# A guard on the softmax of a fused attention and feed-forward kernel: sums judged on GpSimd, and a second path behind a branch

## The chip, the cores and the metric

The kernel runs on one core of a Trainium2 chip. The metric is the device time of one execution in microseconds (us). Engines: TensorE (PE; its weight loads are PEld), VectorE (DVE), ScalarE (ACT), GpSimd (POOL) and SyncE (SP), each with its own stream of instructions, which it takes strictly in order. [...] A trailing q (SPq, POOLq) is the sequencer of an engine, which issues DMAs and handles semaphores.

## The reference

Attention over q, k and v (8 batches, 12 heads, 448 tokens, 64 columns a head), and then a feed-forward layer of width 2048 on the 3584 tokens with 768 columns:

```
scores = (1/8) * q @ k.T
scores = scores - max(scores, over the keys)
attn = exp(scores);  attn = attn / (sum(attn, over the keys) + 1e-9)
x = attn @ v                       # heads put side by side: 3584 x 768
h = x @ w_in;  g = h * sigmoid(h);  out = g @ w_out
```

q, k and v are 0.1 times standard normal draws, so every score is close to 0, every exponential close to 1, and every sum close to 448. Subtracting the maximum changes nothing in exact arithmetic; it keeps the exponentials in range where scores are large.

## The kernel before, in words

**Tiling.** The attention is cut into 24 units (`units`): 8 batches times 3 groups of 4 heads. A unit's keys and queries are loaded (POOL's queue), turned by DVE, multiplied to scores by TensorE (L404), and turned to exponentials in fp16 by ScalarE (`expo`, L442), without the maximum taken off. Two neighbouring units share one tile of exponentials. The sums of the exponentials come from TensorE by products with ones (L495); `inverse` (L541 to L562) turns them on VectorE (L546), takes the reciprocal (L554) and spreads it back (L560); `norm` (L576) multiplies it into the product of exponentials and values (L479). So 24 units times 14 query blocks of 32 give 24 x 14 = 336 inverse sums on each of 128 partitions. In `before`, an inverse lies in a small tile of two rotating buffers (tag `inv`).

**Feed-forward.** Batches 0 to 5 run its first half through `ffn1` (L394, the helper `wide`) with tanh on ScalarE (L602) and a product on VectorE (L640), for the last two of them only in part; batches 4 and 5, and 6 and 7, go in pairs through `pair_product` (L729). Products there are made from sums and differences of blocks: 7 products in the place of 8 (m = 1 to 7 in the order 1, 5, 6, 2, 3, 7, 4). The combined inputs are tiles `sx` (`combine_x`, L676: for b0 = 4 and b0 = 6, m = 1 to 4), the combined weights tiles `tw` or `V` (`combine_w_in`, L709). VectorE adds results in PSUM (`pair_add`, L745: three of them a block, called u, w and v), ScalarE takes copies (L742) and applies silu (L762). The second half runs in the same way over 14 quads of rows (`product`, L394 and for the last quads L799; `combine_g`, L781; `add_in`, L876; `add_out`, L881; `take_out`, L863). The results lie in tiles `ost` and are stored from SyncE's queue, in the last stage from ScalarE's too (L855, and L837 for the last quad). The last columns are copied by `take_half`, by VectorE (L872) and ScalarE (L870).

**Buffers.** Tiles of one tag share a number of buffers. When a tag has no free one, the first instruction that writes the new tile waits until the last reader of an old tile is done. The tag `E` has nine (NE = 9), each of 128 partitions x 3584 bytes. They hold exponentials during the attention; after its end two `sx` of b0 = 4, the four `sx` of b0 = 6 and three `tw` take them.

**Order.** The order of all instructions is written by a planner in the kernel (`class Order`). It plays the kernel through with costs of its own on its own clock (`od.now`), picks for each engine what runs next, and puts a function into `od.out` with the planned time. At the end the list is sorted by time and then by place in the list, and the functions are called; each emits its instructions into the streams:

```
    for _, _, fn in sorted(od.out, key=lambda x: x[:2]):
        fn()
```

The scheduler of the layer below is told to keep this order (`manual_schedule`). TensorE's work goes through `on_pe`; `inv_op` is the list of the planned reciprocals, and `inv_op[-1].done` the planned end of the last. When the program is closed (L1769) the engines drain, meet, and the semaphores are cleared.

Of the kernel before, what the change touches and what calls it, by code (L numbers as in the profile page):

```python
# [10 lines left out]
FP32 = mybir.dt.float32  # L11
AF = mybir.ActivationFunctionType
ALU = mybir.AluOpType
# [74 lines left out]
class Order:  # L88
# [34 lines left out]
    def on_pe(self, op, mode):  # L123
        if mode == "full" and self.attention:
            mode, op.strips = "cols", True
        gap = SWITCH if mode != self.mode else 0.0
        self.mode = mode
        op.busy += gap
        self.start(op)

    def load(self, rows, row_bytes, emit, ring=None, gate=None):
# [52 lines left out]
        return soon  # L184


@with_exitstack
def kernel(
    ctx: ExitStack,
# [4 lines left out]
    moe_w_in: bass.AP,  # L194
    moe_w_out: bass.AP,
    out: bass.AP,
):
    nc = tc.nc

    B, NH, S, D = q.shape  # L200
    DM = NH * D
    DFF = moe_w_in.shape[1]
    HG = 4
    NG = NH // HG
    TPP = S // 32
# [7 lines left out]
    NFF = DFF // 128  # L213
# [16 lines left out]
    NE, NX3, NT_ = 9, 8, 2  # L230
    NXT = 3 * NX3
    NSG, NTMP, NOST = 3, 3, 4
    attn_scale = 1.0 / (D**0.5)

    const = ctx.enter_context(tc.tile_pool(name="const", bufs=1))
    sb = ctx.enter_context(tc.tile_pool(name="sb", bufs=1))
    ps = ctx.enter_context(tc.tile_pool(name="ps", bufs=1, space=bass.MemoryType.PSUM))
# [20 lines left out]
    ones = const.tile([128, 32], FP16, name="ones")  # L258
# [14 lines left out]
    w_out_t = const.tile([128, NFF, DM], FP16, name="w_out_t")  # L273
# [23 lines left out]
    rawk, rawq, KT, QT, E, T, acc, rdn_t, xT, g_t, ost_t = ({} for _ in range(11))  # L297
    sT_t, inv_t = {}, {}
# [242 lines left out]
    def inverse(ns, step, i=0):  # L541
        g0, g1 = units[ns[0]][2:]
        shape = [128, g1 - g0, 32]
        if step == 0:
            sT_t[ns[0]] = sb.tile(shape, FP32, name=f"sT_{ns[0]}", tag="rdn", bufs=2)
            nc.vector.transpose(  # L546
                out=sT_t[ns[0]],
                in_=acc[(ns[0], 0)][:, 0 : 32 * (g1 - g0)].rearrange("p (g i) -> p g i", i=32),
            )
        elif step == 1:  # L550
            inv_t[ns[0]] = sb.tile(
                shape[:2] + [len(ns)], FP32, name=f"inv_{ns[0]}", tag="inv", bufs=2
            )
            nc.vector.reciprocal(  # L554
                out=inv_t[ns[0]], in_=sT_t[ns[0]][:, :, 0 : 32 : 32 // len(ns)]
            )
        else:
            n = ns[i]
            rdn_t[n] = sb.tile(shape, FP32, name=f"rdn_{n}", tag="rdn", bufs=2)
            nc.vector.transpose(  # L560
                out=rdn_t[n], in_=inv_t[ns[0]][:, :, i : i + 1].to_broadcast(shape)
            )  # L562
# [47 lines left out]
    G = const.tile([128, NFF, 2 * S], FP16, name="G")  # L610
# [282 lines left out]
    units = []  # L893
# [3 lines left out]
    NU = len(units)  # L897

    od = Order(SHY)
# [68 lines left out]
    for n in range(NB0 + NG, NU):  # L968
        b, hg = units[n][:2]
# [4 lines left out]
    turned = {"n": 0}  # L974
# [43 lines left out]
    inv_op, norm_op = [], []  # L1018
# [615 lines left out]
    def after_sums(ns, op, nq):  # L1634
        wide = nq / 960.0 + 0.15
        turn = od.add(
            Op("DVE", wide, lambda: inverse(ns, 0), [op] + inv_op[-1:] + norm_op[-4:], B_INV, then=m_ring.back(spot[("a", ns[0], 0)]))
        )
        inv = od.add(Op("DVE", 0.2 + 0.01 * len(ns), lambda: inverse(ns, 1), [turn], B_INV))
        inv_op.append(inv)  # L1640
        for i, n in enumerate(ns):
            rdn_op[n] = [
                od.add(
                    Op(
                        "DVE",
                        wide,
                        lambda i=i: inverse(ns, 2, i),
                        [inv] + norm_op[-4:],
                        B_INV,
                    )  # L1650
                )
            ]
# [24 lines left out]
    def spare():  # L1677
        ready = [(t, 2 * i) for t, i in s_ring.free if t <= od.now]
        ready += [(t, 4 + i) for t, i in m_ring.free if t <= od.now]
        return min(ready)[1] if ready else None  # L1680

    while True:
# [48 lines left out]
        at = spare()  # L1731
        if warm["on"] and at is not None and od.free["PE"] <= od.now and wait > 0.06 and od.now > 0.9:
            each = mm(128) if od.now > COLD else 0.07 if od.now > 6.5 else 0.107
            n = max(1, int((wait - 0.06) / each), int(wait / each + 0.9) * (od.now < 14.0))
            n += MORE0 * (6.5 < od.now < COLD) + 2 * (COLD < od.now < 14.0)
            if warm.pop("first", None):
                n = FIRST
            od.on_pe(Op("PE", n * each, lambda n=n, at=at: run_zeros(n, at)), "full")
        od.now = min(later)
        assert od.now < 2000.0  # L1740
    assert not (qk_seq or av_seq or moe or any(od.wait.values()) or od.pool)
    for _, _, fn in sorted(od.out, key=lambda x: x[:2]):
        fn()


# [28 lines left out]
```

## Time and profile before

| | |
|---|---|
| median of 3 runs | 382.34 us (381.79 to 382.81) |
| the profiled execution | 382.55 us, its span 380.5 us |
| instructions in the span | 12933 |
| PE busy | 373.5 us (98%) |
| DVE busy | 280.2 us (74%) |
| ACT busy | 257.6 us (68%) |
| POOL busy | 85.3 us (22%) |
| granted TensorE clock | 0.999 |

The span goes from the first to the last instruction of the profile; the execution's own time holds 2.05 us more around it. The page has the busy time of each engine, the span in 40 slices of 9.5 us with the busy share of each in tenths, the DMA queues with packets and bytes, the chain of waits that ended last, and groups of instructions by line. The timeline has one line for each run of like instructions: start, duration, engine, line, operation, output and inputs, and in brackets how long the engine had idled before and what released it. Instructions of one engine are pipelined, so a line's duration can reach over the next one's start.

### The profile page before, as it was taken

How to read it: one execution, taken by the hardware profiler on the slowest of the kernel's cores; microseconds unless marked ns; L12 is line 12 of the kernel's file. 1: busy time of each engine (PE TensorE's matmuls, PEld its weight loads, DVE VectorE, ACT ScalarE, POOL GpSimd, SP SyncE). 2: the span in 40 equal slices, each digit the busy share in tenths (PEclk: the TensorE clock that was granted, in tenths of full speed). 3: DMA queues.
4: the chain of work that ended last, by engine and by line, in shares of the span. 5: the costliest groups of instructions: out<-in, count | busy, mean ns of one | idle time of the engine just before them, and what ended most of it. 6: DMA issues, size and time to landing. Idle time of an engine off the chain costs nothing.

```text
span 380.5 us, 12933 instructions
## 1 busy us (share of the span) xinstructions
PE 373.5 (98%) x5516; PEld 192.0 (50%) x5516; DVE 280.2 (74%) x560; ACT 257.6 (68%) x425; POOL 85.3 (22%) x155
## 2 busy tenths in 40 slices
PE   7999999999999999999999999999999999999995
PEld 6433455444455444445444454555556655555653
DVE  5679799999996868997869978789866334556331
ACT  4998854787867787967788787728762259883221
POOL 7537616306042603324240500000000000000000
PEclk9999999999999999999999999999999999999999
DMA  7999999936558843739391712120002330001433
GB/s 103 198 206 190 204 211 183 152 74 91 72 96 135 147 67 44 106 72 169 80 150 26 93 24 72 34 54 0 1 2 69 84 98 2 0 1 39 106 88 103
DMA packets 35961, 34.66 MB, mean 91 GB/s; under 512 B 11968, under 2 KB 35136, under 8 KB 35904
## 3 DMA queue, kind: packets, MB, share of 16 engines
q0 software_dynamic: 25200, 22.82, 40.4%
q1 hardware_dynamic: 10176, 10.53, 10.1%
q8 instruction: 43, 0.70, 0.8%
q10 hardware_dynamic: 528, 0.49, 0.5%
q14 instruction: 14, 0.11, 0.1%
HBM read 45.61 MB, written 11.01 MB: 149 GB/s over the span
## 4 chain that ended last, share of the span: by engine, by line
PE 92%; ACT 3%; DMA 2%; DVE 1%; issue 1%; POOLq 0%
PE banks L394 53%; PE banks L729 15%; PE banks L404 11%; PE banks L479 10%; ACT E L442 3%; PE banks L495 2%; PE banks L799 1%; DMA out_dram<-ost 1%; DMA rk<-in_k_dram 1%; PE banks L1673 0%; DVE ost L881 0%; DVE T L453 0%; PE banks L515 0%; DVE KT L377 0%; DVE rq L387 0%
## 5 line engine op out<-in xcount | busy, mean ns | idle before, releaser
L442 ACT ACTIVATE E<-banks 128x896 f16<-128x896 f32 x168 | 144.1, 919 | 41.2 <-PE banks L404 40.9
L394 PE MATMUL banks<-xT,w_in_t 128*32 128x448 f16 (+1 forms) x1446 | 90.5, 353 | 0.0
L394 PE MATMUL banks<-w_out_t,G 128*32 128x384 f16 (+1 forms) x968 | 67.4, 327 | 0.0
L394 PEld LDWEIGHTS <-G 128*32 128x32 f16 (+1 forms) x1240 | 47.0, 97 | 34.0 <-issue 6.5
L394 PEld LDWEIGHTS <-w_in_t 128*32 128x32 f16 (+1 forms) x1446 | 42.2, 97 | 43.2 <-issue 12.7
L340 POOL DMA_DIRECT2D V<-in_v_dram x84 | 46.0, 560 | 56.0 <-PE banks L479 42.9
L404 PE MATMUL banks<-rq,KT 32*128 32x448 f16 (+1 forms) x768 | 52.1, 362 | 1.5 <-ACT E L442 0.9
L602 ACT ACTIVATE th<-banks 128x448 f16<-128x448 f32 x72 | 37.2, 553 | 15.0 <-PE banks L394 12.5
L640 DVE SCALAR_TENSOR_TENSOR G<-th,banks 128x448 f16<-128x448 f16 (+1 forms) x72 | 39.9, 572 | 4.9 <-ACT th L602 4.5
L863 ACT COPY ost<-banks 128x384 f32<-128x384 f32 x41 | 19.7, 485 | 33.3 <-PE banks L394 17.5
L394 PE MATMUL banks<-D,S 128*32 128x384 f16 (+1 forms) x544 | 38.1, 327 | 0.0
L762 ACT ACTIVATE G<-banks 128x448 f16<-128x448 f32 (+3 forms) x72 | 33.8, 555 | 5.3 <-DVE banks L745 3.5
L479 PE MATMUL banks<-E,V 128*32 128x448 f16 x672 | 35.7, 353 | 0.0
L576 DVE SCALAR_TENSOR_TENSOR xT<-banks,rdn 128x448 f16<-128x448 f32 x48 | 29.2, 618 | 5.6 <-PE banks L479 3.0
L745 DVE TENSOR_TENSOR banks<-banks,q 128x448 f32<-128x448 f32 x28 | 17.6, 632 | 16.6 <-PE banks L729 15.4
L394 PEld LDWEIGHTS <-S 128*32 128x32 f16 (+1 forms) x544 | 20.6, 97 | 14.7 <-issue 3.1
L404 PEld LDWEIGHTS <-KT 32*128 32x128 f16 (+1 forms) x768 | 12.4, 96 | 30.7 <-issue 27.3
L453 DVE TENSOR_TENSOR T<-E,E 128x1792 f16<-128x1792 f16 x22 | 23.8, 1080 | 5.6 <-ACT E L442 5.5
L453 DVE TENSOR_TENSOR T<-T,E 128x1792 f16<-128x1792 f16 x22 | 23.9, 1085 | 5.2 <-ACT E L442 5.0
L317 POOL DMA_DIRECT2D rq<-in_q_dram x25 | 14.0, 559 | 59.8 <-PE banks L404 47.9
L479 PEld LDWEIGHTS <-V 128*32 128x32 f16 x672 | 17.0, 97 | 16.0 <-issue 3.9
L729 PEld LDWEIGHTS <-w_in_t 128*128 128x128 f16 x168 | 16.4, 98 | 15.2
(156 smaller groups left out, 401.3 us busy)
## 6 DMA issues: line engine op xcount, KB each, us to landing
out_dram<-ost SPq DMA_DIRECT2D x200, 48.0 KB, 1.6
rk<-in_k_dram POOLq DMA_DIRECT2D x23, 224.0 KB, 5.4
rq<-in_q_dram POOLq DMA_DIRECT2D x23, 224.0 KB, 5.4
w_out_t<-in_moe_w_out_dram POOLq DMA_DIRECT2D x4, 768.0 KB, 12.6
V<-in_v_dram POOLq DMA_DIRECT2D x42, 64.0 KB, 3.9
V<-in_v_dram POOLq DMA_DIRECT2D x42, 48.0 KB, 4.6
w_in_t<-in_moe_w_in_dram POOLq DMA_DIRECT2D x3, 512.0 KB, 11.2
w_in_t<-in_moe_w_in_dram POOLq DMA_DIRECT2D x6, 256.0 KB, 5.9
```

The costliest lines, as they stand in the source:

```text
L340: nc.gpsimd.dma_start(out=v_of(b, hg0)[32 * x : 32 * (x + 1), at, 0:count, :], in_=v[b, hs].rearrange("h (i g) d -> i h g d", g=TPP)[:, :, ...
L394: nc.tensor.matmul(out=out[at], lhsT=lhsT[:, at], rhs=rhs, **flags)
L404: nc.tensor.matmul(out=pS[p0 : p0 + 32 * (x1 - x0), h % 2, at : at + nq], lhsT=KT[(b, hg)][32 * h : 32 * (h + 1), c, x0:x1, :, e], rhs=QT[ ...
L442: nc.scalar.activation(out=E[(n, w)][0:kr, 2 * y : 2 * y + 2, 0:nk], in_=pS_t[(n, w, y)][0:kr, :, 0:nk], func=AF.Exp, scale=attn_scale,)
L453: nc.vector.tensor_tensor(out=T[n], in0=T[n] if step else E[(n, 0)], in1=E[(n, step + 1)], op=ALU.add,)
L479: nc.tensor.matmul(out=a[32 * h : 32 * (h + 1), 0:nq], lhsT=w, rhs=e[k0:k1, h, at : at + nq], start=start, stop=stop,)
L576: nc.vector.scalar_tensor_tensor(out=x3(b, cc)[:, cc % 3, 32 * g0 : 32 * g1], in0=acc[(n, part)][:, 0:nq], scalar=0.5, in1=rdn_t[n].rearra ...
L602: nc.scalar.activation(out=th, in_=h_t[(b, f, t0)][:, 0 : t1 - t0], func=AF.Tanh)
L640: nc.vector.scalar_tensor_tensor(out=dst[:, f, at + lo : at + hi], in0=th_t[(b, f, t0)][:, lo - t0 : hi - t0], scalar=1.0, in1=h_t[(b, f, ...
L729: nc.tensor.matmul(out=pp_t[(f, PBANK[m])], lhsT=w[:, c, :], rhs=a[:, c, :], start=(c == 0 and m in (1, 6, 5)), stop=(c == 2), skip_group_ ...
L762: nc.scalar.activation(out=o, in_=a, func=AF.Silu, scale=2.0)
L863: nc.scalar.copy(out=ost(qd, i, j), in_=bank(qd, m))
```

## The change

The former kernel function becomes `without_maximum`. The new top function allocates a pool `guard` with a flag of one int32, runs `without_maximum`, which hands back the flag's value as read into a register of every engine, and then stands an `If`: where the value isn't 1, all engines run `with_maximum`, which computes the whole result a second time in fp32, with each query's maximum taken off, and writes `out` again. The inputs of this case give a flag of 1.

In `without_maximum` the inverses of all units are kept in one array `inv_all` of 128 x 336 fp32 in the place of the rotating tiles. `judge` works in three steps, put into the planner's list 20, 28 and 36 us behind the planned end of the last reciprocal: step 0 marks on GpSimd which inverses lie between 1/60000 and 1/64 (two comparisons and a product, 128 x 336 each); step 1 takes the least mark of each partition on VectorE and moves the 128 values into one row by a DMA from GpSimd; step 2 takes the least of the row on VectorE and turns it to the int32 flag on GpSimd. Its scratch tile takes a buffer of the tag `E`. The flag is read (`values_load`, on all engines) at the planned time of the last call of `on_pe`, behind it in the list. The planner's own run isn't changed.

The diff, cut to its core; `with_maximum` is a plain unrolled loop over batches and heads, of which some lines stand here:

```diff
@@ -126,6 +126,7 @@
         gap = SWITCH if mode != self.mode else 0.0
         self.mode = mode
         op.busy += gap
+        self.pe_last = self.now
         self.start(op)
 
     def load(self, rows, row_bytes, emit, ring=None, gate=None):
...
+JUDGED = 20.0
+SUM_LOW, SUM_HIGH = 64.0, 6.0e4
...
+    nc = tc.nc
+    guard = ctx.enter_context(tc.tile_pool(name="guard", bufs=1))
+    flag = guard.tile([1, 1], mybir.dt.int32, name="flag")
+    fine = without_maximum(tc, q, k, v, moe_w_in, moe_w_out, out, guard, flag)
+    with tc.If(fine != 1, preferred_fallthrough_block=False):
+        with_maximum(tc, q, k, v, moe_w_in, moe_w_out, out)
+
+
+def judge(nc, spare, inv, flag, step):
+    n = inv.shape[1]
+    low, high = spare[:, 0:n], spare[:, n : 2 * n]
+    row, one = spare[:, 2 * n : 2 * n + 1], spare[0:1, 2 * n + 1 : 2 * n + 2]
+    line = spare[0:1, 2 * n + 2 : 2 * n + 130]
+    if step == 0:
+        nc.gpsimd.tensor_scalar(
+            out=low, in0=inv, scalar1=1.0 / SUM_LOW, scalar2=None, op0=ALU.is_le
+        )
+        nc.gpsimd.tensor_scalar(
+            out=high, in0=inv, scalar1=1.0 / SUM_HIGH, scalar2=None, op0=ALU.is_ge
+        )
+        nc.gpsimd.tensor_tensor(out=low, in0=low, in1=high, op=ALU.mult)
+    elif step == 1:
+        nc.vector.tensor_reduce(out=row, in_=low, axis=mybir.AxisListType.X, op=ALU.min)
+        nc.gpsimd.dma_start(out=line, in_=row)
+    else:
+        nc.vector.tensor_reduce(out=one, in_=line, axis=mybir.AxisListType.X, op=ALU.min)
+        nc.gpsimd.tensor_copy(out=flag, in_=one)
+
+
+def with_maximum(ctx, tc, q, k, v, moe_w_in, moe_w_out, out):
+    nc = tc.nc
+    B, NH, S, D = q.shape
+    DFF, DM = moe_w_in.shape[1], NH * D
+    NQ, G, NFF = S // 112, S // 32, DFF // 128
...
+    def turned(src, b, h, name):
+        raw = two.tile([32, G, D], FP32, name=f"raw_{name}", tag=f"raw_{name}")
+        nc.sync.dma_start(out=raw, in_=src[b, h].rearrange("(g i) d -> i g d", i=32))
+        t = two.tile([32, 2, S], FP32, name=f"t_{name}", tag=f"t_{name}")
+        for i in range(2):
+            for g in range(G):
+                nc.vector.transpose(
+                    out=t[:, i, 32 * g : 32 * (g + 1)], in_=raw[:, g, 32 * i : 32 * (i + 1)]
+                )
+        return t
...
+    for b in range(B):
+        xT = one.tile([D, NH, S], FP32, name="g_xT", tag="g_xT")
+        for h in range(NH):
+            qT, kT = turned(q, b, h, "q"), turned(k, b, h, "k")
...
+            for c in range(NQ):
...
+                m = two.tile([112, 1], FP32, name="g_m", tag="g_m")
+                nc.vector.tensor_reduce(
+                    out=m, in_=s[:, 0:S], axis=mybir.AxisListType.X, op=ALU.max
+                )
+                nc.sync.dma_start(out=row[:, 112 * c : 112 * (c + 1)], in_=m)
...
+                e = two.tile([112, S], FP32, name="g_e", tag="g_e")
+                nc.scalar.activation(out=e, in_=s[:, 0:S], func=AF.Exp, scale=1.0 / D**0.5)
+                for o, w in ((x, vt[:, c]), (total, ones)):
+                    nc.tensor.matmul(
+                        out=o[:, 0:S], lhsT=w, rhs=e, start=(c == 0), stop=(c == NQ - 1)
+                    )
...
+        for f in range(NFF):
...
+            nc.scalar.activation(out=gate[:, f], in_=hid[:, 0:S], func=AF.Silu)
...
+            nc.sync.dma_start(out=out[at : at + 112], in_=o)
...
+def without_maximum(
...
+    inv_all = guard.tile([128, NG * B, TPP], FP32, name="inv_all")
...
         elif step == 1:
-            inv_t[ns[0]] = sb.tile(
-                shape[:2] + [len(ns)], FP32, name=f"inv_{ns[0]}", tag="inv", bufs=2
-            )
+            b, hg = units[ns[0]][:2]
+            at = NG * b + hg
+            whole = inv_all[:, at : at + len(ns)].rearrange("p n g -> p (n g)")
+            inv_t[ns[0]] = whole.rearrange("p (g n) -> p g n", n=len(ns))
...
     assert not (qk_seq or av_seq or moe or any(od.wait.values()) or od.pool)
+    spare_t = []
+
+    def judged(step):
+        if step == 0:
+            spare_t.append(
+                sb.tile([128, 2 * NU * TPP + 130], FP32, name="judge", tag="E", bufs=NE)
+            )
+        judge(nc, spare_t[0], inv_all.rearrange("p n g -> p (n g)"), flag, step)
+
+    read = []
+    why = "compared only, no address is made of it"
+
+    def read_flag():
+        read.append(nc.values_load(flag, skip_runtime_bounds_check_because=why))
+
+    od.out.append((od.pe_last, len(od.out), read_flag))
+    for step in range(3):
+        at = inv_op[-1].done + JUDGED + 8.0 * step
+        od.out.append((at, len(od.out), lambda step=step: judged(step)))
     for _, _, fn in sorted(od.out, key=lambda x: x[:2]):
         fn()
+    return read[0]
```

## The prediction

> **What bounds the kernel now.** I read the page's parts 1 to 3 first, then the chain of waits, then the timeline by engine from 245 us to 290 us (where the sums are judged) and from 372 us on (where the flag is read), and last the rows of the line that closes the program, L1769.
>
> The page:
>
> ```profile
> PE 373.5 (98%) x5516; PEld 192.0 (50%) x5516; DVE 280.2 (74%) x560; ACT 257.6 (68%) x425; POOL 85.3 (22%) x155
> ...
> POOL 7537616306042603324240500000000000000000
> ...
> q8 instruction: 43, 0.70, 0.8%
> ```
>
> TensorE is busy 98% of the span, and in the chain of waits it holds 92%. So a microsecond of TensorE idleness anywhere before the last stage is a microsecond of the result; it is not won back. GpSimd does nothing after slice 23 (its last DMA issue ends near 217 us). The third line is the code itself: with q14 it makes 57 packets and 0.81 MB for 12,933 instructions, 63 bytes each. The engines fetch their code by DMA while they run, in pieces of 0.70 MB / 43 = 16.3 KB, about 260 instructions.
>
> The timeline of VectorE and of TensorE around 274 us, where the change's buffer matters:
>
> ```profile
> 272.92 0.63 DVE L745 TENSOR_TENSOR banks<-banks,q 128x448 f32<-128x448 f32 x1
> 273.46 0.85 DVE L676 TENSOR_TENSOR sx<-xT,sx 128x1344 f16<-128x1344 f16 x1
> 275.02 0.63 DVE L745 TENSOR_TENSOR banks<-banks,q 128x448 f32<-128x448 f32 x1 [0.71 <-PE banks L729]
> ```
> ```profile
> 274.82 0.73 PE L729 MATMUL banks<-sx,tw 128*128 128x448 f16 x3
> 275.39 0.73 PE L729 MATMUL banks<-xT,w_in_t 128*128 128x448 f16 x3
> 275.95 0.73 PE L729 MATMUL banks<-xT,tw 128*128 128x448 f16 x3
> ```
>
> The L676 at 273.46 is the last of the tiles `sx` (the one for b0 = 6, m = 4), and VectorE idles 0.71 us behind it. The L745 at 275.02 ends at 275.65, and TensorE's third group starts 0.30 us later, on the bank that it read.
>
> The end of the kernel, first the timeline, then the rows of L1769:
>
> ```profile
> 374.43 3.01 SPq L837 DMA_DIRECT2D out_dram<-ost  x3
> 374.94 1.48 PE L799 MATMUL banks<-D,G 128*128 128x192 f16 x16
> 375.14 0.48 ACT L863 COPY ost<-banks 128x384 f32<-128x384 f32 x1 [2.12 <-PE banks L799]
> 376.52 0.36 DVE L872 COPY ost<-banks 128x192 f32<-128x192 f32 x1 [2.12 <-DMA out_dram<-ost]
> 376.91 0.32 ACT L870 COPY ost<-banks 128x192 f32<-128x192 f32 x1 [1.29 <-DVE ost L872]
> 377.26 0.66 ACTq L837 DMA_DIRECT2D out_dram<-ost  x1
> ```
> ```profile
> L1769 SPq EVENT_SEMAPHORE  x10: 17/28/28, 377.5 to 380.4; - x10
> ...
> L1769 SPq DRAIN  x3: 7/7/7, 379.6 to 379.9; - x3
> ```
>
> TensorE ends at 376.42, two copies follow, the last store is issued until 377.92, and SyncE waits for its landing until 379.6. From there to 380.45 the engines meet twice and the semaphores are cleared: a closing round of 0.85 us.
>
> The profiled execution took 382.55 us (2.05 us around its span of 380.5), 0.21 us above the median of 382.34. I sum against 382.55 and take 0.21 off at the end.
>
> **The change, part by part.**
>
> *Inverse kept in one array.* The 14 reciprocals (L554, 0.31 us) write 28 or 14 columns elsewhere; number and shape stay. Two rotating buffers go, and no wait stood on them (the list of waits has none for `inv`). Cost 0.
>
> *Three GpSimd operations on 128x336 f32.* The program order puts them 20 us behind the last inverse, but GpSimd is in no queue with anything then, so they start when their inputs and their buffer allow: the last reciprocal ends at 248.4, the E buffers of the last unit are free when its products (L479) end at 252.9. No such operation is in the trace. Bounds for one: 0.10 us (GpSimd's memset of one column) and 1.26 us (twice VectorE's 0.63 us for 128x448 f32). I take 0.7, so 2.1 us, 253 to 255. Nobody waits for them before 276. Cost 0 by that row. Beside VectorE work at the same time both bounds stay: nothing, or up to 1.0 us, if the L709s at 252.98 to 254.4 (three, 0.55 us each) are held up by them and VectorE, which has no idle time from 251.5 to 261.5, hands half on. I take 0 and keep 1.0. [...]
>
> *The buffer of these operations.* It is an E buffer (nine of them), and this is the first term that I count. After the last exponential nine tiles take E buffers, in the order of their first writes: sx of b0 = 4 twice (243.70, 245.47), two tw (253.9, 260.4), sx of b0 = 6 (263.04, 268.32), a tw (269.09), sx (270.92, 273.46). Nine for nine: none waits. Judge's tile is asked for at 248.4 + 20 = 268.4 by the planner's clock, some 2 to 5 us ahead of the last two. So it makes ten, and the last, the L676 at 273.46, gets the buffer of the first, which is free only when the last product with it is done: that is the triple sx,tw at 274.82, ending at 275.55. Then L676 starts at 275.6 instead of 273.46, and behind it in VectorE's order the L745 starts 0.77 later (the step from one L676 to the next operation at 263.04), at 276.37 instead of 275.02. It ends at 277.0, TensorE's group of 275.95 starts at 277.15 or up to 277.3: a hole of 1.2 to 1.35 us. VectorE then has the idle 1.01 us ahead of 279.16 to catch up, so nothing adds to it. **I count 1.2 us**; bounds 0 (the tile comes after 273.46, or finds a free buffer) and 1.35.
>
> *Step 1: a reduction of 128x336 f32 on VectorE and a DMA of 128x4 bytes from GpSimd.* Between 0.31 (L554, 28 columns) and 0.63 us (L745, 448 columns); I take 0.5, near 276.4, in front of the same 1.01 us of idleness. With the lateness above, 1.35 + 0.5 stands against the 0.71 + 1.01 us that VectorE idled; what is left over, 0.1 us, falls on the three L781 and not on L745. Cost 0, bound 0.5. The DMA costs GpSimd 0.56 us (L340), lands after 1.5 us (the least store) to 5.9 us (the longest store), so by 283, and is wanted 8 us behind step 1, at 284.4.
>
> *Step 2: a reduction of 1x128 and a copy of one element.* Between 0.07 and 0.31 us on VectorE (a memset, L554), inside the run of L781 from 283.27 to 290; the half sums made there are read over a microsecond later. Cost 0, bound 0.3.
>
> *The flag read into a register on all five engines*, in program order right behind the last matmuls are emitted: on VectorE between the L881 ending at 374.42 and the L872 at 376.52, on ScalarE between its DMA issues (ending 373.9) and the L863 at 375.14, on SyncE between two stores, on TensorE last. Not in the trace; between 0.02 us (a semaphore event) and 2.3 us (a round trip of a DMA). Cover: 2.1 us on VectorE, 1.2 us on ScalarE; at 2.3 the L863 would be 1.1 late, its store would land near 379.0, still ahead of 379.4. So 0, bound 0.2.
>
> *The comparison and the branch*, the second term. All engines but GpSimd must pass some code of the second path: it is unrolled, and by the diff VectorE has 120 instructions a head for 96 heads, TensorE 28 matmuls a head and 2,560 for the second half, ScalarE 96 x 4 + 128 = 512, SyncE over 800. These exceed the 260 instructions of a code piece, so where the untaken path lies between the body and the closing lines, the closing code isn't in when the branch asks for it. Price of one fetch: a 16.3 KB packet holds its DMA engine 0.8% x 16 x 380.5 / 43 = 1.13 us, and a store takes 1.5 us at the least from issue to landing. Bounds 1.13 and 1.13 + 2.3 = 3.4; **I take 2.6** (1.13 + 1.5). What is it beside? The counts of semaphores must agree on both ways, and those of stores can't be set before the stores have landed; so I place the branch behind the landing at 379.6, and 0.2 us for reading and comparing (ten semaphore events of 0.02). The closing round of 0.85 then follows as before.
>
> [...]
>
> Sum: 382.55 + 1.2 + 0.2 + 2.6 = 386.55; less 0.21, **386.3 us**.
>
> **The rivals.**
>
> *The fetch beside the landing* (0.25). If engines branch without waiting for stores, ScalarE, the last, branches at 377.92 + 0.1 and has its code at 380.6, 1.0 us behind 379.6. With the buffer 2.2: 384.5. For it: SyncE alone waits for the stores today.
>
> *No fetch* (0.15). The closing code lies next to the branch. The buffer's 1.2 is left, or with a second closing round 1.2 + 0.85: 383.5 to 384.4.
>
> *Two fetches or an extra round* (0.11). If each way around the second path is a jump of its own, or the round of 0.85 is also run ahead of the branch: 1.2 + 0.2 + 0.85 + 2.6 to 1.2 + 0.2 + 2 x 2.6, up to 389; at 3.4 a fetch, with both, 391.
>
> *Not slower* (0.12). One mechanism: all that is added ends under the last store's landing and the late buffer isn't met. [...] It decides if the target is at hand and judge's tile is placed behind the L676 of 273.46 (then only GpSimd waits for its buffer, to 275.6, and step 1 by about 1 us in VectorE's idle time). 382.4.
>
> That the flag were out of range and the second path run is excluded by the inputs: sums of 448 exponentials of values near 0 are near 448, inside 64 to 60,000.
>
> **How the numbers follow.** Forecast 0.37, the rivals as given. The range goes from 383.3 to 389.6: it leaves out the last rival and the upper end of the third, some 0.18. 0.3% is 1.15 us, about what measurement tells from no change. Nothing removed was on the path, so faster has 0.02; within 0.3% has the last rival and a little of the no-fetch case, 0.13; slower 0.85.
>
> **What would show it.** Right: the L676 of 273.46 starts behind the triple sx,tw and TensorE has a hole of about 1.2 us there, with TensorE's last matmul ending near 377.6; behind the last store's landing, 2 to 4 us in which no engine works and instruction packets move. Wrong: TensorE ending at 376.4 (no late buffer), a hole near 253 to 261 (GpSimd in VectorE's way), VectorE waiting for GpSimd near 276 or 284, or a span whose closing round still begins at 379.6 plus TensorE's delay (no fetch).

## The result, and the profile after

The changed kernel took **387.14 us** (median of 4 runs, 386.63 to 388.05) against 382.33 us for the kernel before on the same chip (4 runs, 381.79 to 382.81): 1.0129 times as long, 95% interval 1.0105 to 1.0152. Its profiled execution took 386.63 us, with a span of 384.8 us at a granted clock of 0.995.

The page of after, parts 1 to 3, for the lines that were read before:

```profile
PE 374.1 (97%) x5516; PEld 192.6 (50%) x5516; DVE 280.8 (73%) x562; ACT 257.7 (67%) x425; POOL 91.1 (24%) x160
POOL 7538517206051605142411400030020000000000
q8 instruction: 45, 0.74, 0.7%
q14 instruction: 20, 0.16, 0.1%
```

TensorE has the same 5,516 matmuls and 0.6 us more of them: the body of the kernel is as it was. GpSimd's digits 3 and 2 in the 27th and 30th slices are the new judging. The instruction queues moved 8 packets more (45 + 20 against 43 + 14). The chain of waits, which held 92% TensorE before, holds next to nothing here: it has the last two copies (0.7 us) and ends at the first of them, whose wait the profile puts down to TensorE's branch (PEq L210, below). That is no sign of the loss itself: e11_later below has the same loss, and its chain is 91% TensorE again. One has to go on by rows.

So I measured the **tail**, from the end of TensorE's last matmul to the end of the span. The timeline of after, the rows that set its start:

```profile
374.13 1.48 PE L966 MATMUL banks<-D,G 128*128 128x192 f16 x16
375.71 0.36 DVE L1039 COPY ost<-banks 128x192 f32<-128x192 f32 x1 [2.12 <-PEq L210]
376.45 0.65 ACTq L1004 DMA_DIRECT2D out_dram<-ost  x1
```

TensorE ends at 374.13 + 1.48 = 375.61. Before, it ended at 374.94 + 1.48 = 376.42 with the span's end at 380.5, a tail of 4.08 us. After has 384.8 - 375.61 = **9.19 us**. All of the loss, 5.1 us, lies behind the last matmul. (The body's end itself differs by 0.8 us here and lies between 375.6 and 378.0 in the profiles of this study, so one profile's span doesn't compare kernels; tails and medians do.)

In the tail, the rows of the `If` (L210), then those of the closing lines (L1956): number, least/median/longest duration in ns, first and last start in us.

```profile
L210 SPq EVENT_SEMAPHORE  x8: 17/17/17, 376.8 to 380.2; - x8
L210 PEldq COMPARE_BRANCH  x2: 90/2132/4173, 374.4 to 375.8; - x2
...
L210 SPq COMPARE_BRANCH  x2: 38/46/53, 376.7 to 380.3; - x2
L210 ACTq COMPARE_BRANCH  x2: 38/50/61, 377.1 to 377.3; - x2
```
```profile
L1956 SPq EVENT_SEMAPHORE  x14: 17/28/28, 383.2 to 384.8; - x14
...
L1956 SPq DRAIN  x3: 7/7/7, 384.0 to 384.3; - x3
L1956 DVEq DRAIN  x2: 10/45/80, 379.3 to 384.3; - x2
L1956 ACTq DRAIN  x2: 8/44/81, 379.9 to 384.3; - x2
L1956 PEldq DRAIN  x2: 8/40/73, 380.0 to 384.3; - x2
```

Each engine has two branches: the comparison, and behind it, in the arm that is run when the flag is 1, a jump over the second path. Between the two, SyncE settles the eight store lanes on which the second path would have counted; that takes until the last store has landed (376.8 to 380.2). It jumps at 380.3, and its next instruction, the first of the closing list, starts at 383.2: **2.9 us** in which no engine starts an instruction, and in which instruction packets move (one of q14 in each half microsecond from 380.5 to 381.5). The other engines had paid the same earlier: VectorE comes back at 379.3, ScalarE at 379.9, TensorE at 380.0, all before SyncE. Then SyncE goes through the closing list of lane waits from 383.2 to its drain at 384.0, 0.8 us, and the closing round follows as before, 0.8 us.

And the landing itself is later. The DMA issues between 374 and 385 us (KB each, median us from issue to landing):

```profile
q14 instruction: 6, 0.05, 1.4%
q8 instruction: 2, 0.03, 1.3%
...
out_dram<-ost SPq DMA_DIRECT2D x1, 96.0 KB, 3.7
out_dram<-ost ACTq DMA_DIRECT2D x1, 96.0 KB, 3.5
```

The same view of before, from 374 to 381 us, has no instruction packet, and for these two stores:

```profile
out_dram<-ost SPq DMA_DIRECT2D x1, 96.0 KB, 2.0
out_dram<-ost ACTq DMA_DIRECT2D x1, 96.0 KB, 2.1
```

The queue q8 carries TensorE's code (0.70 MB before, for 2 x 5,516 instructions of some 64 bytes) in pieces of 16 KB; q14 carries the other engines' in 8 KB (in e6_sp_only below, where SyncE alone fetches, two q14 packets move in the tail and none of q8).

The tail by stretch, in us behind the last matmul's end: lanes settled at 4.7 (before, where the closing waits ran under the landing, drain at 3.2): +1.5. Code fetch: +2.9. Second round of waits: +0.8. Closing round: the same. Together 5.2 for the 5.1 measured.

### The profile page after: what moved, and what is told of

The parts are those of the page before. It is cut to its first block, busy times and chain, and to the rows that moved or that the text cites. A ratio compares the mean times of both kernels' runs of the same rounds, so it can differ in the third digit from the quotient of the medians.

```text
span 384.8 us, 12974 instructions
## 1 busy us (share of the span) xinstructions
PE 374.1 (97%) x5516; PEld 192.6 (50%) x5516; DVE 280.8 (73%) x562; ACT 257.7 (67%) x425; POOL 91.1 (24%) x160
```

## The experiments

The theory: the body is free, and the tail pays three times, for a late landing (code on the DMA engines that carry the last stores, TensorE's above all), for SyncE's fetch behind the landing, and for waiting twice. The rival that I had forecast, a hole in TensorE through the buffer, would put part of the loss into the body. All medians, against 382.3 to 382.5 us for before on the same chips; "landing" is the last store of SyncE / of ScalarE, "SyncE" the time from its last branch to its next instruction; ratio with its 95% interval. The span is given to 0.1 us, so a tail's second digit isn't sure.

| | median | ratio | tail | landing | SyncE |
|---|---|---|---|---|---|
| before | 382.33 | | 4.08 | 2.0/2.1 | |
| after | 387.14 | 1.0105 to 1.0152 | 9.19 | 3.7/3.5 | 2.9 |
| e1_no_branch | 382.30 | 0.9984 to 1.0013 | 4.08 | 2.0/2.1 | |
| e2_small_body | 382.68 | 0.9997 to 1.0019 | 4.47 | 2.5/2.6 | 0.2 |
| e3_true_first | 384.65 | 1.0041 to 1.0080 | 6.75 | 2.9/2.4 | 2.8 |
| e4_pool_queue | 384.07 | 1.0021 to 1.0053 | 5.37 | 3.5/3.4 | 0.2 |
| e5_one_head | 384.81 | 1.0037 to 1.0076 | 6.65 | 3.4/3.3 | 0.2 |
| e6_sp_only | 387.16 | 1.0069 to 1.0155 | 8.28 | 2.0/2.3 | 2.6 |
| e7_pe_only | 383.51 | 1.0013 to 1.0040 | 5.33 | 3.4/3.3 | 0.2 |
| e8_hint | 384.75 | 1.0038 to 1.0072 | 6.45 | 2.9/2.9 | 2.8 |
| e9_short_path | 383.94 | 1.0028 to 1.0057 | 5.82 | 3.0/2.9 | 0.2 |
| e10_hint_other | 383.85 | 1.0023 to 1.0058 | 5.19 | 2.9/2.7 | 0.2 |
| e11_later | 387.17 | 1.0083 to 1.0144 | 8.98 | 3.8/3.7 | 2.6 |

One sum for the whole: before's median less its tail is 378.2 us. 378.2 plus the tail gives the median of every row within 0.7 us, and of most within 0.3. What a variant costs is what its tail costs.

**The judging without the branch.** The flag is computed, and neither read nor compared; the second path is left out.

```diff
-    fine = without_maximum(tc, ..., out, guard, flag)
-    with tc.If(fine != 1, preferred_fallthrough_block=False):
-        with_maximum(tc, q, k, v, moe_w_in, moe_w_out, out)
+    without_maximum(tc, ..., out, guard, flag)
```

> The sums are judged as in the changed kernel, but the flag is neither read nor branched on, and there is no second path. Theory (all of the loss is behind the last matmul: branch, fetch, waits): 382.3 us within 0.5, and from the end of TensorE's last matmul to the end of the span 4.1 us as before. Rival (judging costs the body, by the late buffer or by GpSimd beside VectorE): 383.3 or more, with TensorE's last matmul later by that.

Measured 382.30 us, no difference from before, and before's tail. GpSimd's three operations, the buffer, both reductions, the DMA: together nothing that can be measured. The rival falls.

**A second path of four instructions.**

```diff
-        with_maximum(tc, q, k, v, moe_w_in, moe_w_out, out)
+        with tc.tile_pool(name="small", bufs=1) as small:
+            t = small.tile([112, 768], FP32, name="t")
+            nc.vector.memset(t, 0.0)
+            nc.scalar.copy(out=t[:, 0:1], in_=t[:, 1:2])
+            nc.sync.dma_start(out=out[0:112], in_=t)
```

> The second path is replaced by four instructions (clear a tile, one copy, one store), so the code behind the branch lies close by; the second path's computation is left out. Theory (the distance of the closing code makes the loss): no fetch, the last stores land 2.1 us after their issue, and only the repeated list of waits of 0.75 us stays: 383.2 us, the tail behind the last matmul 5.0 us. Rival (a conditional costs this by itself, through its waits and rounds): 387, tail 9.2.

382.68 us, tail 4.47: flag, comparison and branch add 0.4 us to the tail, and the median can't be told from before's. It is less than expected because this arm settles one lane instead of eight, and SyncE's closing waits (from 377.8, drain at 380.0) run under the landing again. (SyncE's branch at 376.9 stands ahead of its last store here, which it goes on to issue at 377.2.) Reading and comparing aren't the price; what lies in the second path is.

**The second path placed right behind the comparison**, so that the way past it is a single far jump ahead of the lane waits.

```diff
-    with tc.If(fine != 1, preferred_fallthrough_block=False):
+    with tc.If(fine != 1, preferred_fallthrough_block=True):
```

> Only the order of the code: the second path stands right behind the comparison, the untaken arm behind it, next to the closing code. Theory (SyncE's fetch of 2.9 us comes after it has waited for the stores, and is as long if it comes before): SyncE jumps at once, its fetch runs beside the stores' landing, 387.1 - 2.9 = 384.2 us, tail 6.3 us. Rival (the fetch is wanted a second time behind the waits, or the time is not a fetch): 387.

384.65 us. SyncE branches at 377.8 and settles its first lane at 380.6: the fetch is as long as before, 2.8 us, but lies beside the landing. Both rounds of waits come behind it, 0.6 and 0.7 us. TensorE's packet came at 376 to 376.5 here, ahead of the last stores' packets, and they landed in 2.9/2.4; of SyncE's 2.9 the issue itself took 1.2, where it took 0.5 in before.

**The second path's DMAs on GpSimd's queue**, in all its six calls, of which one is shown:

```diff
-        nc.sync.dma_start(out=raw, in_=src[b, h]...)
+        nc.gpsimd.dma_start(out=raw, in_=src[b, h]...)
```

> All DMAs of the second path are issued by GpSimd in the place of SyncE, so SyncE has nothing to skip and no counts to settle; GpSimd, which takes its branch near 288 us, skips them long before the end. Theory (the loss is SyncE's: fetch 2.9 and repeated waits 0.75, and the landing 1.4 later because TensorE's, VectorE's and ScalarE's code comes by the same DMA engines): 387.1 - 3.65 = 383.5 us, tail 5.5, the last stores landing after 3.5 us as in the changed kernel. Rival for the landing (it was late by chance or by SyncE's branch): 2.1 us and 382.3. Rival for all (each engine's branch is behind the landing): 387.

384.07 us, tail 5.37. The rows of its `If` and of its closing lines for SyncE:

```profile
L210 SPq COMPARE_BRANCH  x2: 38/46/53, 376.8 to 376.9; - x2
```
```profile
L1956 SPq EVENT_SEMAPHORE  x14: 17/28/28, 377.1 to 381.0; - x14
...
L1956 SPq DRAIN  x3: 7/7/7, 380.2 to 380.5; - x3
```

SyncE has no second path to pass: no lanes between its two branches, no fetch behind them. Its closing waits run under the landing from 377.1. The other three still fetch, back at 379.3 to 380.1, ahead of the drain at 380.2. What remains of the tail, +1.3 against before, is the landing (3.5/3.4).

**The second path cut to one batch and one head**, the head also in the first half of its feed-forward part, a third loop that isn't shown. (It would then recompute only a part; it isn't run.)

```diff
-    for b in range(B):
+    for b in range(1):
-        for h in range(NH):
+        for h in range(1):
```

> The second path is cut to one batch and one head, so it uses all lanes of SyncE's stores but is short: the closing code lies about 30 instructions away for SyncE and under 190 for the others. The second path's result would be wrong beyond that; it isn't run. Theory (distance): no fetch, stores land after 2.0 to 2.6 us, then the list of 13 waits is gone through a second time, 0.75 us: tail behind the last matmul 4.1 + 0.1 + 0.75 = 5.0 us, 383.2 us. Rival (settling the lanes is the cost, not the fetch): 386 or more.

384.81 us against 383.2 expected. SyncE jumps at 381.3 and goes on at 381.5: past code this short it is held 0.2 us, and the fetch is gone. The miss is in the rest. TensorE keeps 172 matmuls, 28 for the head and 16 and 128 for the two halves of the feed-forward part. With their weight loads, at some 64 bytes an instruction, I estimate 22 KB, more than one 16 KB piece. Its branch takes 3,990 ns, and the landing is 3.4/3.3, 0.8 above the upper end that I had put; and the closing waits took 1.2 us instead of 0.75.

**Long code on SyncE alone, and on TensorE alone.** The body of the `If` is 600 loads, or 5,000 matmuls.

```diff
-        with_maximum(tc, q, k, v, moe_w_in, moe_w_out, out)
+            for _ in range(600):
+                t = many.tile([32, 14, 64], FP32, name="t", tag="t")
+                nc.sync.dma_start(out=t, in_=q[0, 0].rearrange(...))
```
```diff
-        with_maximum(tc, q, k, v, moe_w_in, moe_w_out, out)
+            for i in range(5000):
+                nc.tensor.matmul(out=o[:, 0:448], lhsT=t[:, 0:128], rhs=t, ...)
```

> The second path is 600 loads issued by SyncE and nothing else (its computation is left out), so SyncE alone has far closing code. Theory (the landing is late because the other engines' code comes by the same DMA engines): stores land after 2.0 to 2.6 us, then SyncE's fetch of 2.9 us and the 0.75 us of waits: tail 4.1 + 0.1 + 2.9 + 0.75 = 7.8 to 8.3 us, 386.0 us. Rival (the landing is late for another reason): 3.5 us, tail 9.2, 387.1.

> The second path is 5000 matmuls on one tile (its computation is left out), so TensorE alone has far closing code, and SyncE has nothing to settle. Theory: TensorE's fetch ends at about 380.0, near where the closing round begins anyway. If its code packets meet the last stores: landing 3.4 us, tail 5.4, 383.6 us; if the meeting needs the other engines' code too: 2.0 to 2.6, tail 4.1 to 4.5, 382.5. Rival (any engine's fetch adds its full length to the end): 385 or more.

These two were to separate the terms. SyncE alone (the rows of the `If`, of the last stores and of the closing lines, and the DMAs from 374 to 386 us):

```profile
L210 PEldq COMPARE_BRANCH  x2: 85/132/180, 376.7 to 376.9; - x2
L210 SPq COMPARE_BRANCH  x2: 38/46/53, 378.3 to 380.3; - x2
```
```profile
L1007 SPq DMA_DIRECT2D out_dram<-ost x3: 545/562/571, 375.9 to 383.0; - x3
...
L1007 ACTq DMA_DIRECT2D out_dram<-ost x1: 662/662/662, 380.2 to 380.2; - x1
```
```profile
L1959 SPq EVENT_SEMAPHORE  x13: 17/28/28, 383.6 to 386.1; - x13
L1959 SPq DRAIN  x3: 7/7/7, 385.3 to 385.6; - x3
```
```profile
q14 instruction: 2, 0.02, 0.5%
...
out_dram<-ost ACTq DMA_DIRECT2D x1, 96.0 KB, 2.3
out_dram<-ost SPq DMA_DIRECT2D x1, 96.0 KB, 2.0
```

TensorE alone:

```profile
L210 PEldq COMPARE_BRANCH  x2: 90/2040/3990, 375.2 to 376.6; - x2
L210 SPq COMPARE_BRANCH  x2: 38/46/53, 377.4 to 377.5; - x2
```
```profile
q8 instruction: 2, 0.03, 1.0%
q14 instruction: 1, 0.01, 0.2%
...
out_dram<-ost SPq DMA_DIRECT2D x1, 96.0 KB, 3.4
out_dram<-ost ACTq DMA_DIRECT2D x1, 96.0 KB, 3.3
```

With long code on SyncE alone, SyncE fetches and TensorE does not (its branch takes 180 ns). But the order of SyncE's instructions isn't that of after: its branch stands ahead of its last store. It settles the eight lanes until 380.3, jumps, and is back at 382.9, after 2.6 us. Only then does it issue the last store, at 383.0, which lands 2.0 us later; the wait for that landing fills most of the closing waits, from 383.6 to the drain at 385.3. ScalarE's store, too, starts only at 380.2, when SyncE has settled its lane. So the tail of 8.28 has the size expected and another make-up, and the landing (2.0/2.3) shows only that stores that meet no code of TensorE's land nearly as before. The median is 1.1 us above the forecast; the four runs scatter from 385.99 to 388.81, and this profile's body ended late, at 377.92.

With long code on TensorE alone SyncE loses nothing, TensorE's branch (3,990 ns against 180) ends at 380.6, ahead of SyncE's drain at 380.8, and the landing alone makes the tail 5.33, at the size expected. In this run a q8 packet starts between 378 and 378.5, among the last stores' packets, and one of q14 beside it; in after a q8 packet starts between 377 and 377.5, where it takes 15.4% of 16 engines for 0.5 us, that is 1.2 us of one engine, and some store packets trail until 379.5. That these are the ones queued on the same DMA engine is inferred; the views name no engine for a packet.

**A branch prefetch hint** on SyncE, TensorE, VectorE and ScalarE behind the reading of the flag, on top of the order of e3.

```diff
+        tc.mark_branch_hint_location(
+            "second", hint=read[0] * -1 + 1,
+            engines=[ENG.SP, ENG.PE, ENG.DVE, ENG.Activation],
+        )
```

> As with the second path first, with a hint behind the flag's load on TensorE, VectorE, ScalarE and SyncE that the untaken arm's code will be wanted, so that it is fetched 2 to 4 us ahead of the branch. Theory (the price is a fetch on demand, which may run ahead beside other work): SyncE is held 0.5 us at most, what is left is the repeated list of waits: tail 5.0 to 5.6, 383.2 to 383.8 us. Rival (the hint fetches nothing, or the packets now meet the last stores): as the second path first, 384.65.

384.75 us, as e3. The hint ran on SyncE at 377.7, 1.7 us ahead of its branch at 379.4, and the next instruction came at 382.2: 2.8 us, as without. TensorE's branch alone was shorter, 3,517 ns against 3,977 in e3.

**A second path short on every engine**: e5's, with one block of each half of the feed-forward part and without the products for the maximum. By the edit that leaves 19 matmuls (the expectation says 23) and 10 loads and stores in all; all eight lanes stay. Of the edit one loop is shown.

```diff
-                for f in range(NFF):
+                for f in range(1):
```

> The second path is cut further than in e5_one_head: one head without its maximum, one block of each half of the feed-forward layer, 23 matmuls in all, and still ten DMAs on SyncE, so that all eight lanes have to be settled. The rest of its computation is left out. Theory (the last stores are late because TensorE's code is fetched, and its code was still far in e5_one_head): no engine fetches, stores land after 2.0 to 2.6 us, then the second list of waits of 0.75 to 1.2 us: tail 4.1 + 0.2 + 0.75 to 1.2, with up to 0.5 for the landing, 5.1 to 6.0 us; 383.6 us. Rival (settling the lanes makes the stores late): landing 3.4, tail 6.6, 384.8.

383.94 us, tail 5.82, in the range expected. No engine fetches (TensorE's branch 180 ns, SyncE 380.2 to 380.4); the second round of waits, 380.4 to 381.1, is left with 0.7 us. The landing is 3.0/2.9 though, with one q14 packet and none of q8: a late landing doesn't need TensorE's code. The views of e9 by half microseconds, from 378 and from 379 us:

```profile
...
q14 instruction: 1, 0.01, 8.0%
```
```profile
q10 hardware_dynamic: 9, 0.01, 3.7%
q1 hardware_dynamic: 3, 0.00, 2.3%
```

The q14 packet starts among the packets of the last two stores (q1 and q10), and from 379 to 379.5 twelve of those still move, as many as in after; in before it is one. In e2 one q14 packet moves between 374 and 386 us, and the landing is 2.5/2.6; in e1, with 2.0/2.1, there is one too, and neither is placed more closely. So in every run with a late landing that was read by half microseconds (after, e3, e7 to e11) a code packet lies near the last stores' packets, of TensorE's queue or of the other, and before, where none moves from 374 to 381 us, has 2.0/2.1.

**The hint with the other value**, with e3's order and e4's queues.

```diff
-            hint=read[0] * -1 + 1, engines=[SP, PE, DVE, Activation]
+            hint=read[0] * 1, engines=[PE, DVE, Activation]
```

> All DMAs of the second path on GpSimd's queue as in e4_pool_queue, the second path first as in e3_true_first, and a hint on TensorE, VectorE and ScalarE with the value turned round against e8_hint (1 where the flag is 1). Theory A (the hint of e8 named the wrong side): VectorE and ScalarE, which have 2 to 4 us between hint and branch, are through their branch in under 1.5 us in the place of 2.6 to 3.1; TensorE has no lead and still takes 4. Theory B (a hint brings nothing here): they take 2.6 to 3.1 as before. The time under both, since TensorE's code and the landing decide: tail 5.3 to 5.6, 384.0 us.

383.85 us, tail 5.19. VectorE still needs 3.5 us from its branch to its next instruction, ScalarE 2.8 (3.5 and 3.0 in e3): on SyncE, VectorE and ScalarE the hint saved nothing in either sense. TensorE's branch took 3,402 ns here and 3,517 in e8, against 3,977 to 4,293 in the six runs without a hint in which it fetches. That is half a microsecond or more with either value, in one profile each, and not on the path. What ends last here is ScalarE's fetch: the last store, issued at 377.04, has landed 2.7 us later, at 379.7, and SyncE's drain comes at 380.5, when ScalarE is back. This kernel has the lowest median of those that keep the whole guard, 1.5 us above before; e4's 384.07 can't be told from it.

**The judging 10 us later in the plan**, so that its tile is asked for behind the last `sx`.

```diff
-JUDGED = 20.0
+JUDGED = 30.0
```

> Judging is put 30 in the place of 20 us behind the last inverse on the planner's clock, so its tile is the tenth to ask for one of the nine E buffers. Theory (VectorE's L843 at 273.34 waited for the buffer of the first of them, whose last reader is the triple of matmuls ending at 273.30): L843 no longer waits, and GpSimd's first comparison, at 252.2 before, starts when that triple ends, near 273.3 on the same clock; the time stays at 387.1, since neither is on the path. Rival (the wait at L843 has another cause): it is still there, and GpSimd starts near 252.

387.17 us, as after. The buffers can be seen. GpSimd's, VectorE's and TensorE's timelines of this run:

```profile
274.30 1.20 POOL L220 TENSOR_SCALAR judge<-inv_all 128x336 f32<-128x336 f32 x1 [57.30 <-PE banks L896]
```
```profile
273.73 0.85 DVE L843 TENSOR_TENSOR sx<-xT,sx 128x1344 f16<-128x1344 f16 x1
```
```profile
273.38 0.73 PE L896 MATMUL banks<-sx,tw 128*128 128x448 f16 x3
```

Now it is GpSimd that waits: it has been idle since 217 and starts at 274.30, 0.19 us behind the end of the triple sx,tw (273.38 + 0.73 = 274.11), and the last `sx` starts without idleness. Whichever of the two is asked for later waits for the same triple, and neither costs anything.

## Why the prediction was right or wrong

The time came out 0.8 us above the forecast and inside the range, and the fetch that was forecast is there. But the sum was right by errors that cancel, which is luck: a term of 1.2 us that isn't there stands against two of 0.8 and 1.5 us that were left out.

**The buffer term (1.2 us) failed**, in the step "that is the triple sx,tw at 274.82". The rest of its chain holds: judge's tile makes ten, and the last `sx` waits for the first one's buffer. Timelines of after, VectorE and TensorE:

```profile
272.38 0.63 DVE L912 TENSOR_TENSOR banks<-banks,q 128x448 f32<-128x448 f32 x1
273.34 0.86 DVE L843 TENSOR_TENSOR sx<-xT,sx 128x1344 f16<-128x1344 f16 x1 [0.33 <-PE banks L896]
274.48 0.63 DVE L912 TENSOR_TENSOR banks<-banks,q 128x448 f32<-128x448 f32 x1 [0.28 <-PE banks L896]
```
```profile
272.57 0.73 PE L896 MATMUL banks<-sx,tw 128*128 128x448 f16 x3
...
274.28 0.73 PE L896 MATMUL banks<-sx,tw 128*128 128x448 f16 x3
...
275.41 0.73 PE L896 MATMUL banks<-xT,tw 128*128 128x448 f16 x3
```

The buffer's last reader is the triple two lines earlier, at 272.57, ending at 273.30 (the one at 274.28 is before's 274.82); there are two lines "sx,tw" in that stretch, and I took the later one without proving which `sx` it reads. The L843 (before's L676) then waits 0.33 us, not 2.1, and the idleness behind it shrinks from 0.71 to 0.28. TensorE has no hole: the group of 275.95 in before starts at 275.41 here, 0.54 us earlier, and so does every group around it, from 247.84 (247.30 here), ahead of the judging, to 289.59 (289.05), behind it. So neither GpSimd's work nor the buffer moved TensorE. The e1 run puts the term at 0, and e11 confirms the buffer. (The sign named for this, TensorE's end at 377.6 against 376.4, could not have decided it, since that end scatters from 375.6 to 378.0.)

**The fetch (2.6 us) held**, in place and size: one fetch, behind the landing, 2.9 us here and 2.6 to 2.9 in all runs where SyncE passes long code; 0.2 where it doesn't (e2, e4, e5, e7, e9, e10). In e5, e6, e7 and e9 whether an engine fetches goes with the length of its own code alone: behind 600 loads SyncE is held 2.6 us and TensorE's branch takes 180 ns (e6), behind 5,000 matmuls TensorE's takes 3,990 ns and SyncE goes on after 0.2 (e7); with 172 matmuls TensorE's takes 3,990 ns (e5), with 19 it takes 180 (e9).

**Two terms were missing.** "A closing round of 0.85 follows as before" held, but I overlooked that the closing list's waits, which before ran under the landing, would be gone through a second time behind the fetch: 0.8 us (e9 has it without a fetch, 0.7). And I let the stores land as before: +1.5 us. The packet that holds a DMA engine for 1.13 us stood in my own sum as the price of the fetch, and I didn't ask what else that engine had to carry. So 2.9 + 0.8 + 1.5 in the place of 0.2 + 1.2 + 2.6, about 1.2 more; 0.8 of it shows in the medians, and the rest is within the scatter of the body's end.

**The costs taken as nothing held** (e1). The operations on GpSimd were mis-sized, with no effect:

```profile
252.21 1.08 POOL L220 TENSOR_SCALAR judge<-inv_all 128x336 f32<-128x336 f32 x1 [36.03 <-PE banks L645]
253.35 1.13 POOL L223 TENSOR_SCALAR judge<-inv_all 128x336 f32<-128x336 f32 x1
254.56 0.89 POOL L226 TENSOR_TENSOR judge<-judge 128x336 f32<-128x336 f32 x1
...
285.05 1.99 POOL L232 CAST flag<-judge 1x1 int32<-1x1 f32 x1 [6.89 <-DVE judge L231]
```

3.1 us instead of 2.1, where forecast, and nobody waits. Beside them VectorE is held up a little: the first L876 takes 0.66 us (0.56 before), the next pair 1.28 (1.02):

```profile
252.44 0.66 DVE L876 TENSOR_TENSOR V<-w_in_t 128x768 f16<-128x768 f16 x1
253.02 1.28 DVE L876 TENSOR_TENSOR tw<-w_in_t 128x768 f16<-128x768 f16 x2
```

0.36 us in all, against the bound of 1.0 kept for it; in e11, where GpSimd is idle at that time, they are back at 0.56 and 1.02. e1 shows that it doesn't reach the end. Step 1 took 0.50 us (as put), step 2 0.27, the load of the flag 0.48 to 0.54 us on four engines and 0.97 on SyncE, all under their cover. A comparison with its branch took 38 to 61 ns on SyncE, VectorE and ScalarE in after.

**The rivals.** "Fetch beside the landing" isn't what the change does, but e3 and e4 make it so: 384.65 and 384.07 us for the 384.5 forecast, though without its buffer term and with late landings in its place. Its sum has 0.1 us for ScalarE's branch at 377.92, a term that no run shows; in after ScalarE's two branches took 38 and 61 ns. "Not slower" failed on its first condition, since the target isn't at hand (SyncE is held 2.9 us behind its jump); its second, judge's tile behind the last `sx`, wasn't met either (e11 makes it so), but what should follow from it, a buffer that costs nothing, held. "No fetch" is what e2 and e9 make of it: 382.68 and 383.94 us for the 383.5 to 384.4 forecast, again without the buffer term. "Two fetches or an extra round" was right in that something is gone through twice, 0.8 us, behind the one fetch.

What stays open: why the hint brings nothing on three engines, and whether it is what shortened TensorE's branch; by what way a code packet delays the stores, for which the runs show that they go together and no more; and why the closing waits took 1.2 us in e5 instead of 0.75 (two q8 and two q14 packets move between 374 and 386 us there, and their place wasn't shown).

## What to carry to other kernels

In these runs a conditional that is never taken was paid where its code must be passed: not by the test (0.4 us of tail with a small body), but by the fetch of what lies behind a long body (2.6 to 2.9 us on SyncE), by the waits that settle the counts of the arm not run (a second round of 0.7 to 1.2 us), and with code packets among the last stores (landings of 3.3 to 3.8 us instead of 2.0 to 2.3). Look which engine holds the last waits of the kernel and give it nothing in the untaken arm (moving the second path's DMAs off SyncE took 3.1 of the 4.8 us back), or put the far jump ahead of the waits. Look, too, where the branch stands among the last stores: in e6 one store had to wait for the fetch. And where a buffer wait is forecast, trace the reader by tile and order, not by a like-named group near it: a wait of 0.3 us and one of 2.1 look the same in the plan.

## What the hardware showed that was not expected

In these runs a far jump cost each engine its own time: 2.6 to 2.9 us on SyncE, 2.6 on ScalarE and 3.1 on VectorE in after, 4.2 on TensorE, where it is shown as the branch's own duration (4,173 ns in after), while on the others it is a gap behind a branch of 38 to 61 ns. A single 16 KB piece of TensorE's code among the last stores, with an 8 KB piece or two of another engine's, went with landings of 3.3 to 3.8 us (after, e7, e11) instead of 2.0 to 2.3 (before, e6); an 8 KB piece alone went with 3.0/2.9 (e9).

A copy of one element from fp32 to int32 took GpSimd 1.99 us in after, e1, e4, e6 and e7, longer than either comparison of 128x336 (1.08 and 1.13 in after), and 0.18 us in e11:

```profile
296.07 0.18 POOL L232 CAST flag<-judge 1x1 int32<-1x1 f32 x1 [7.08 <-DVE judge L231]
```

In after the copy lasts from 285.05 to 287.04, and VectorE has a run of operations on `G` and `S` (L948) from 284.92 to 287.00; in e11 VectorE is at work on PSUM banks (L1043) during the copy. So the 1.99 us look like waiting for VectorE and not like the price of the copy; no run was made to show it.
